# First superblock: the up-projection begun in halves of 256 columns for two chunks instead of four, with a new order of issue

## The chip, the cores and the metric

The kernel runs on one core of a Trainium2 chip. The metric is the time of one execution on the device, in microseconds (us). Before the change it is 470.64 us, the median of three runs (470.19 to 471.09).

## What is computed

The reference is a transformer block with adaptive layer norm: a linear-attention half and an MLP half, each with a residual, on 2048 tokens of width 512, in float32.

```python
sa, ca, ga, sb, cb, gb = split(silu(c) @ w_mod)            # six rows of 512
h = layernorm(x) * (1 + ca) + sa
q, k, v = h @ wqkv                                         # 32 heads of 16
phi(t) = concat(softmax(t @ w_phi), softmax(-t @ w_phi))   # per head, 32 features
o = phi(q) @ (phi(k).T @ v) / (phi(q) @ sum(phi(k)) + 1e-6)
x = x + ga * (o @ wo)
h = layernorm(x) * (1 + cb) + sb
y = layernorm(h)                                           # the MLP normalises again
x = x + gb * (gelu(y @ w1 + b1) @ w2 + b2)                 # w1: 512 x 1376
```

## The kernel before

Every product is taken as three float32r matmuls on high and low parts (`mm3`: high by high, high by low, low by high), so a tile of 128 rows with four slices of the contraction is 12 matmuls.

The tokens are 8 blocks of 256 (two tiles of 128). Two stages follow each other. In the first the weights are loaded and folded (`fold`), and block by block the keys, values and queries are projected (`pk`, `pv`, `pq`), the key features made (`ek`) and summed into one state (`pkv`, 32 small matmuls a tile). In the second the attention output of a block is formed and the MLP runs over four superblocks, each of two blocks (512 tokens). The names that matter here, for the stretch between the stages:

- `t` transposes the normalised query features of blocks 0 and 1 on TensorE (`qp`), and ScalarE copies them out (`qT`, `attn_t`, L800). `o` multiplies them with the state (`po`, L818), `w` with the output weights (`pw`, L844).
- `la`, `lb`, `lc` (L851 to L871) are the residual and the two layer norms of a tile. VectorE does sums, statistics and scalings on `pw`; ScalarE copies the residual out (`x1`) and writes the result `h2`; each reciprocal root (`rsb`, `rsc`) is one GpSimd operation between two VectorE ones.
- `y` (`attn_y`, L880) transposes `h2` of a block on TensorE (`yp`, 8 matmuls); ScalarE writes the high part (`yT0`), VectorE the low part (`yT1`).
- `u` (`up`, L916) is one chunk of the up-projection: 128 of the 1376 features for the 512 tokens of a superblock, 12 matmuls of 512 columns into `pg`; then the gelu on ScalarE and the split into `g`. `d` is a chunk of the down-projection (`py`, 12 matmuls).
- `w_prep` (L606) loads a pair of chunks of `w2` into `ws`, multiplies it on GpSimd, copies it on ScalarE (`w2a`, `w2b`) and subtracts on GpSimd. `w1` is prepared likewise (`w1s` to `w1`).

A chunk of the first superblock needs both blocks 0 and 1. For the first `AHEAD` chunks (L202) it is done in two halves, so that the half of block 0 can run before block 1 has its `yT`:

```python
n = 256 if b == 0 and fc < AHEAD else 512
for j in range(0, 512, n):
    if n < 512:
        nc.item(f"u{j // n}")
```

The halves are items `u0` and `u1`, whole chunks `u`. Both halves of a chunk write one PSUM bank, and its gelu follows the second.

What sets the order: the program first records every instruction into queues by part and item (`Later`, L220), and `issue` (L237) then emits them in the order of the table `ISSUE` (L87), one string for each of the 13 parts. `u0.p` is the TensorE part of the next `u0`, `.a` ScalarE, `.v` VectorE, `.g` GpSimd, `.s` a DMA on the queue of SyncE; a `-` takes the item from the part before, a `+` from the part behind. Each engine executes its instructions in that order and waits for what the next one needs. `SLOTS` (L46) says which of the 19 working buffers (`buf`), the 8 PSUM banks and the small tiles each new tile takes; a tile waits until the last user of its buffer is done. All matmuls, activations and transfers are recorded under one line, L217, so that the profile tells them apart by tile.

Of the kernel before, what the change touches and what calls it, by code (L numbers as in the profile page):

```python
# [59 lines left out]
    "mxk": "1010101110101010",  # L60
    "smk": "0110010111011011",
    "rck": "1010010111101101",
    "mxq": "10110010",
    "smq": "00000000",
    "rcq": "10100020",
    "den": "00101110",
    "rd": "10111011",
    "st6b0": "10100110",
    "stb0": "10111101",
    "veb0": "10010101",  # L70
    "rsb0": "11001011",
    "st6c0": "01000110",
    "stc0": "10111100",
    "vec0": "00100100",
    "rsc0": "00101000",
    "nmc0": "10010111",
    "st6b1": "11110101",
    "stb1": "10000110",
    "veb1": "11111110",
    "rsb1": "00010101",  # L80
    "st6c1": "10000001",
    "stc1": "10111010",
    "vec1": "00110110",
    "rsc1": "00100101",
    "nmc1": "00000111",
# [40 lines left out]
pk1.p -k0.v -k1.a --bg.g -k0.v -k1.v pk0.p h.a -v0.v v1.v k1.v -v0.a -k0.g +d0.s h.a k1.v ----e.s h.a h.a f.a -m0.p
--bg.g k0.v f.a -m1.p k1.v m0.p k1.v pv1.p +w1.s -k1.v +w1.s k1.a --v1.v f.g -v1.v k0.v v1.v k0.v f.g k1.v
""",
    """
pk1.p -v1.a -----e.v --k1.g ---bg.a --v1.a -k0.v -k0.a -k1.v pk0.p ----v0.v k1.v +lp0.s -k1.g -k0.v --v1.v --bg.g  # L130
-k0.v -m1.p w1.a k0.v m1.p k1.v -pv0.p w1.a d0.s v1.v k0.v w1.s -k0.g k0.v v0.v k1.v k0.v -v0.v pv0.p w1.g k0.a
-v0.a k0.v w1.g k0.v pv1.p k1.v v0.a +a0.v k1.a v0.v v1.v k1.v k0.g q1.p v1.a k1.v w1.a +a0.v k1.g ---v0.v m0.p
+a0.g m2.p m3.p w1.g kT.a d1.s d1.s z.p z.a kf.p +a0.g q0.p z.a q1.a a0.g q1.p a1.g a0.v -----e.v a0.v --bg.s q2.p
q1.a a1.g +a0.a kf.v a0.v q0.a a1.v q2.p a0.g a1.v a0.g a0.g +a0.g a0.v +a0.v q0.p a1.g a0.g a1.g a0.v a1.g a0.g
a1.v q4.p q0.a --bg.s x0.s q2.a a1.g +a0.g t01.p a1.g +a0.a t01.p t00.p t00.p +a0.v q4.p q4.a a1.g t01.a +a0.v t00.a
t01.a t00.a +a0.g q2.a o01.p q2.s o00.p w1.s t10.p q0.s o00.a t11.p o01.a +a0.g o00.v t10.p t11.p o01.v w00.p t10.a
+a0.v q4.a t11.a q4.s --bg.g +a0.v t10.a t11.a w1.a o11.p la00.v o10.p la00.a -bg.g w01.p x1.s o10.a la00.v o11.a
o10.v la00.v o11.v +a0.g -bg.a la00.v la00.v la00.g w11.p +a0.g la01.v +a0.g w1.g lb00.v la01.a +a0.v la01.v lb00.v
w10.p la11.v w1.s q1.s la01.v lb00.v la11.a la01.v la01.v +lp1.s la01.g w2.s la11.v -bg.g lb01.v q3.p la11.v lb01.v
la10.v +a0.g lb01.v la11.v la10.a lb00.v lb01.v la11.v lb00.g lb01.g q3.p la10.v la11.g lc00.v la10.v lc01.v la10.v  # L140
lc01.a la10.v la10.g lb11.v +a0.g lc00.a lb10.v q3.a y0.p q3.a lb11.v y0.p y0.a +a0.g lb10.v q3.s y0.a y0.v --bg.a
lb10.v y0.v
""",
    """
u0.p -w1.a -lb11.v -lb10.v -lb11.v a0.v -lb10.g -lb11.g u0.p a0.v ---bg.g -lc10.v -lc11.v a0.v a0.s -lc10.a a1.v
a0.s u0.p -lc11.a a0.s a1.v a0.s a1.g -y1.p -y1.p -y1.a u0.p --v0.v a0.v a1.g -y1.a -y1.v a0.s a1.g -y1.v a1.a a0.s
u1.p a0.s a1.g a0.s u1.p -w1.g +lp0.s u.a u.a u1.p u.a u.v a0.s u.a a1.v a0.s -w2.g d.p -w1.s u.a d.p u.v u.a d.p
u.v d.p a1.g a1.a d.p d.p -w2.a a1.v d.p a1.g d.p a1.v d.p x0.s a1.v u1.p -w2.g a1.v o01.p o00.p +a0.v d.p o00.a
a1.g -w2.s o01.a o00.v d.p a1.g a1.g +a0.g u.p a1.v o01.v u.a a1.g a1.g d.p a1.g w01.p a1.v u.a +a0.v u.a -w1.a u.v
u.a -w2.g a1.v d.p la01.v a1.s d.p a1.v la01.a a1.s w00.p u.v +a0.g -w2.a a1.s a1.v a1.s -w2.g la01.v a1.s a1.s  # L150
# [45 lines left out]
d.p u.v d.p d.p d.p u.p d.p u.a d.p u.a d.p u.v d.p u.p u.p u.a u.a u.v d.p u.a d.p u.a u.p u.v d.p u.a d.p u.a d.p  # L196
u.a u.a d.p u.a u.a u.a u.v d.p d.p d.p d.p d.p out.v d.p out.s d.p out.v d.p out.s d.p out.v d.p out.s out.v out.v
out.s out.s
""",
]  # L200
W2A = 6
AHEAD = 4  # L202
NT = 2
BUFS = 19
ALIGN = 64
NE = 2


# [963 lines left out]
```

## Time and profile before

| | us |
|---|---|
| median of three runs | 470.64 |
| the profiled execution | 470.68 |
| its span | 468.9 |
| TensorE busy | 462.5 (99%) |
| VectorE busy | 314.1 (67%) |
| GpSimd busy | 279.7 (60%) |
| ScalarE busy | 235.6 (50%) |

The ends of matmuls are modelled, so a busy TensorE may hold short waits; the chain of waits gives the dense rate. The stretch in which the two stages meet lies between 140 and 205 us of the span.

### The profile page before, as it was taken

The page shows a single profiled execution, that of the slowest core. Times are in us where ns is not written, and L with a number is a line of the kernel's source. Part 1 is how long each engine was busy: PE and PEld are TensorE (multiplying, and loading weights), DVE is VectorE, ACT ScalarE, POOL GpSimd, SP SyncE. Part 2 cuts the span into 40 slices and gives each one's busy share as a digit, 9 for nine tenths or more (in the row PEclk, how much of TensorE's full clock was granted, in tenths as well). Part 3 has the DMA queues.
Part 4 walks back from the last instruction along what each step waited for, and adds up shares of the span by engine and source line. Part 5 has one row for each costly group of instructions (what it writes and reads, how often), then busy time and mean ns, then how long its engine had stood idle before and what let it go on. Part 6 is the DMA issues. An engine that isn't in the chain of part 4 may idle for free.

```text
span 468.9 us, 8567 instructions
## 1 busy us (share of the span) xinstructions
PE 462.5 (99%) x3313; PEld 375.2 (80%) x3313; DVE 314.1 (67%) x610; ACT 235.6 (50%) x383; POOL 279.7 (60%) x233
## 2 busy tenths in 40 slices
PE   9999999999999999999999999999999999999996
PEld 5888888888878878988787878788788788788884
DVE  4999989998848389578885869795873282211113
ACT  2777686855541555758537672166533224422221
POOL 0485859879899989999879975663740010400000
PEclk9999999999999999999999999999999999999999
DMA  8999639636622446937636838168337205100002
GB/s 293 401 263 296 148 78 244 220 65 217 205 64 89 141 174 228 223 112 163 191 97 135 223 113 202 48 110 196 118 76 178 87 0 135 46 22 24 0 1 89
DMA packets 81033, 67.00 MB, mean 143 GB/s; under 512 B 52560, under 2 KB 68320, under 8 KB 80736
## 3 DMA queue, kind: packets, MB, share of 16 engines
q1 hardware_dynamic: 80992, 66.46, 50.1%
q8 instruction: 26, 0.43, 0.4%
q14 instruction: 15, 0.12, 0.1%
HBM read 44.41 MB, written 22.03 MB: 142 GB/s over the span
## 4 chain that ended last, share of the span: by engine, by line
PE 92%; DVE 3%; issue 1%; ACT 1%; DMA 1%; DVEq 0%; ACTq 0%
PE pg L217 26%; PE py L217 26%; PE pv L217 9%; PE pk L217 9%; PE pq L217 7%; PE pw L217 7%; PE warm L217 2%; PE pkv L217 2%; PE fold L217 1%; DVE pw L217 1%; PE po L217 1%; DMA pq_dram<-qs 1%; ACT qT L217 1%; DVE st6c L217 1%; PE zp L217 0%
## 5 line engine op out<-in xcount | busy, mean ns | idle before, releaser
L217 PE MATMUL pg<-yT,w 128*128 128x512 f32 (+1 forms) x528 | 115.5, 370 | 0.7 <-DVE yT L217 0.4
L217 PEld LDWEIGHTS pg<-yT,w 128*128 128x128 f32 x528 | 92.9, 188 | 18.2 <-DVE yT L217 0.6
L217 ACT ACTIVATE pg<-pg,blob 128x512 f32<-128x512 f32 x44 | 29.1, 661 | 106.5 <-PE pg L217 104.3
L217 DVE TENSOR_TENSOR g<-pg,g 128x512 fp32r<-128x512 f32 x40 | 27.2, 684 | 66.9 <-ACT g L217 66.7
L217 PE MATMUL py<-w2a,g 128*128 128x512 f32 x288 | 71.9, 392 | 0.0
L217 PEld LDWEIGHTS py<-w2a,g 128*128 128x128 f32 x288 | 53.5, 188 | 13.4 <-issue 1.6
L217 PE MATMUL py<-w2b,g 128*128 128x512 f32 x192 | 47.2, 390 | 0.0
L217 PE MATMUL pv<-wvh,hT 128*128 128x512 f32 x192 | 45.8, 392 | 0.0
L217 PE MATMUL pk<-wk,hT 128*128 128x512 f32 x192 | 45.6, 391 | 0.0
L217 PE MATMUL pw<-wo,oT 128*128 128x512 f32 x192 | 45.6, 390 | 0.0
L217 PE MATMUL pq<-wq,hT 128*128 128x512 f32 x192 | 45.2, 390 | 0.0
L217 POOL TENSOR_TENSOR ez<-eq,zb 128x1024 f32<-128x1024 f32 x15 | 36.4, 2440 | 13.2 <-PE pg L217 6.1
L217 PEld LDWEIGHTS py<-w2b,g 128*128 128x128 f32 x192 | 35.9, 188 | 8.1 <-issue 0.7
L217 PEld LDWEIGHTS pw<-wo,oT 128*128 128x128 f32 x192 | 35.9, 188 | 7.8 <-issue 0.4
L217 PEld LDWEIGHTS pq<-wq,hT 128*128 128x128 f32 x192 | 35.9, 188 | 7.4
L217 PEld LDWEIGHTS pv<-wvh,hT 128*128 128x128 f32 x192 | 35.7, 188 | 7.5
L217 PEld LDWEIGHTS pk<-wk,hT 128*128 128x128 f32 x192 | 35.8, 188 | 7.3
L217 POOL TENSOR_TENSOR ek<-ek,rck 128x1024 f32<-128x1024 f32 x16 | 31.0, 1947 | 4.3 <-ACT vf L217 1.6
L217 POOL TENSOR_TENSOR eq<-eq,rcq 128x1024 f32<-128x1024 f32 x15 | 28.9, 1939 | 0.2
L217 ACT ACTIVATE g<-pg 128x512 fp32r<-128x512 f32 x40 | 24.0, 599 | 9.5 <-DVE stc L217 2.8
L217 POOL TENSOR_TENSOR rsb<-veb,mhalf 128x1 f32<-128x1 f32 x16 | 8.8, 550 | 30.3 <-DVE veb L217 30.3
L217 POOL TENSOR_TENSOR yT<-yf,yT 128x256 fp32r<-128x256 f32 x24 | 17.1, 744 | 15.2 <-ACT yT L217 15.2
(154 smaller groups left out, 802.4 us busy)
## 6 DMA issues: line engine op xcount, KB each, us to landing
et_dram<-eb SPq DMA_DIRECT2D x48, 128.0 KB, 2.8
eT<-et_dram SPq DMA_DIRECT2D x12, 512.0 KB, 5.5
xt<-in_x SPq DMA_DIRECT2D x8, 512.0 KB, 6.4
wms<-in_wmodT SPq DMA_DIRECT2D x8, 512.0 KB, 5.9
x<-in_x SPq DMA_DIRECT2D x8, 512.0 KB, 3.8
out<-x SPq DMA_DIRECT2D x15, 256.0 KB, 2.1
nt_dram<-nb SPq DMA_DIRECT2D x24, 128.0 KB, 3.3
hd<-nt_dram SPq DMA_DIRECT2D x6, 512.0 KB, 4.2
```

Source lines behind the costliest of these rows:

```text
L217: return lambda *a, **k: self.later.hold(self.letter, lambda: f(*a, **k))
```

## The change

`AHEAD` goes from 4 to 2: chunks 2 and 3 of the first superblock are one item `u` with 12 matmuls of 512 columns instead of `u0` and `u1` with 12 of 256 each. TensorE has 48 matmuls of 256 columns less and 24 of 512 more. The work of the other engines is the same, but for two table loads less on ScalarE. The whole of `ISSUE` and of `SLOTS` is new.

```diff
 SLOTS = {
     "buf":
-    "32eg91ai750d4gf6cf8ehcd187ga30203dh540b52ca0i999hba44571a6i7b8gag3fii0729f4c2fe569d1ehch8d61bg59801c"
+    "cd732950ega7f8146ba9acbah2g53i18b8id6c71470ide31ac60h0gd354ch66b4e95391gi6g8b8f2h275f0i6aeacd471b3h2"
...
-AHEAD = 4
+AHEAD = 2
```

On TensorE, where the first superblock begins: `yp` are the transposes of block 0 (`h2_438`) and of block 1, `pg_506`, `pg_508`, `pg_517` are the chunks 0, 1 and 2. Before:

```order
L217 MATMUL yp_480<-blob_106,h2_438 128x128 x4
L217 MATMUL pg_506<-yT0_475,w1_376 128x256
...
L217 MATMUL pg_508<-yT0_475,w1_376 128x256
...
L217 MATMUL pg_517<-yT0_475,w1_376 128x256
...
L217 MATMUL yp_502<-blob_106,h2_499 128x128 x4
L217 MATMUL yp_503<-blob_106,h2_499 128x128 x4
```

After:

```order
L215 MATMUL yp_480<-blob_106,h2_438 128x128 x4
L215 MATMUL pg_506<-yT0_475,w1_376 128x256
...
L215 MATMUL yp_502<-blob_106,h2_499 128x128 x4
L215 MATMUL yp_503<-blob_106,h2_499 128x128 x4
L215 MATMUL pg_508<-yT0_475,w1_376 128x256
```

Three halves (36 matmuls) stood between the two groups of transposes; now one half (12 matmuls) does.

On GpSimd, around the layer norms of block 0: `rsb0_431` is the first reciprocal root, `ws_349` and `w2a_348` prepare `w2`, `w1_377` prepares `w1`, `dz`, `den` and `rcq` belong to the attention of block 2. Before:

```order
L217 TENSOR_TENSOR ez_523<-eq_515,zb_116 128x1024
L217 TENSOR_TENSOR ws_324<-ws_324,gbb_115 128x1024
L217 TENSOR_TENSOR ws_349<-ws_349,gbb_115 128x1024
L217 TENSOR_TENSOR dz_521<-dz_521,rcq_520 128x128
L217 TENSOR_TENSOR rsb0_431<-veb0_430,mhalf_108 128x1
L217 TENSOR_TENSOR den_524<-dz_521 128x64
L217 TENSOR_TENSOR den_524<-den_524,deps_109 128x64
L217 TENSOR_TENSOR w1_377<-w1s_386,w1_377 128x4x256
L217 TENSOR_TENSOR rsb1_464<-veb1_463,mhalf_108 128x1
```

After:

```order
L215 TENSOR_TENSOR ez_523<-eq_515,zb_116 128x1024
L215 TENSOR_TENSOR ws_349<-ws_349,gbb_115 128x1024
L215 TENSOR_TENSOR dz_521<-dz_521,rcq_520 128x128
L215 TENSOR_TENSOR w1_377<-w1s_386,w1_377 128x4x256
L215 TENSOR_TENSOR den_524<-dz_521 128x64
L215 TENSOR_TENSOR rsb0_431<-veb0_430,mhalf_108 128x1
L215 TENSOR_TENSOR den_524<-den_524,deps_109 128x64
L215 TENSOR_TENSOR ws_324<-ws_324,gbb_115 128x1024
L215 TENSOR_TENSOR rcq_520<-rcq_520,rd_525 128x128
L215 TENSOR_TENSOR rsb1_464<-veb1_463,mhalf_108 128x1
```

`w1_377` moved ahead of `rsb0_431`, and `ws_324` behind it, ahead of `rsb1_464`. By the new `SLOTS`, `ws_349` now takes the buffer that the first `qT` of block 0 held, so its load waits for the `po` matmuls that read that `qT`; the two `qT` of block 1 take the buffers of two `eq` tiles that the `qp` transposes read.

## Rows read from the trace of the kernel before

**Rows 1.** The page: busy us (share of the span) and instructions, by engine.

```profile
PE 462.5 (99%) x3313; PEld 375.2 (80%) x3313; DVE 314.1 (67%) x610; ACT 235.6 (50%) x383; POOL 279.7 (60%) x233
```

**Rows 2.** Stretches: busy us (instructions) by engine, granted clock, DMA share, GB/s.

```profile
24.39:140.00 115.61, 115.07 (x1486) 95.12 (x1486) 101.81 (x214) 74.35 (x122) 96.23 (x63) 1.00 0.61 178
140.00:189.00 49.00, 47.88 (x301) 39.10 (x300) 37.02 (x67) 23.86 (x39) 45.35 (x38) 1.00 0.49 159
205.00:340.00 135.00, 135.00 (x705) 108.38 (x704) 106.14 (x184) 75.65 (x114) 101.05 (x95) 1.00 0.57 143
```

**Rows 3.** The chain that ended last: start us, us, engine and tile.

```profile
86.16 5.69 PE pv L217 x24
...
189.66 5.75 PE pg L217 x48
195.41 6.52 PE py L217 x27
...
203.36 1.02 PE po L217 x32
...
216.21 2.72 PE pg L217 x12
```

**Rows 4.** Timeline of TensorE, 160 to 190: start, us, tile, count, idle before.

```profile
161.81 1.97 PE L217 MATMUL qp<-blob,eq 128*128 128x128 f32 x16
163.53 3.01 PE L217 MATMUL pw<-wo,oT 128*128 128x512 f32 x12
166.93 1.58 PE L217 MATMUL po<-qT,gab 64*32 64x256 f32 x32 [0.39 <-ACT qT L217]
168.44 8.46 PE L217 MATMUL pw<-wo,oT 128*128 128x512 f32 x36
176.73 5.61 PE L217 MATMUL pq<-wq,hT 128*128 128x512 f32 x24
...
184.33 4.46 PE L217 MATMUL pg<-yT,w 128*128 128x256 f32 x35 [0.43 <-DVE yT L217]
```

**Rows 5.** Timeline of ScalarE, 150 to 192.

```profile
165.79 1.57 ACT L217 ACTIVATE qT<-qp 128x512 f32<-128x512 f32 x3 [0.95 <-DMA pq_dram<-qs]
...
186.58 1.45 ACT L217 ACTIVATE h<-pw,nmc,rsc 128x512 f32<-128x512 f32 x2 [0.74 <-DVE nmc L217]
```

**Rows 6.** DMA of the tile ws, 135 to 190: issue to landing.

```profile
DMA to landing us min/median/max: 3.7/4.2/6.7
```

**Rows 7.** Timeline of GpSimd, 150 to 192.

```profile
164.79 4.73 POOL L217 TENSOR_TENSOR ws<-ws,gbb 128x1024 f32<-128x1024 f32 x2
169.48 0.46 POOL L217 TENSOR_TENSOR dz<-dz,rcq 128x128 f32<-128x128 f32 x1
170.98 0.56 POOL L217 TENSOR_TENSOR rsb<-veb,mhalf 128x1 f32<-128x1 f32 x1 [1.04 <-DVE veb L217]
171.50 0.29 POOL L217 TENSOR_TENSOR den<-dz 128x64 f32<-128x64 f32 x1
172.12 2.39 POOL L217 TENSOR_TENSOR w<-w1s,w 128x1024 fp32r<-128x1024 f32 x1
```

**Rows 8.** Timeline of VectorE, 150 to 192.

```profile
172.10 0.75 DVE L217 SCALAR_TENSOR_TENSOR pw<-pw,rsb,sbb 128x512 f32<-128x512 f32 x1
...
183.60 0.67 DVE L217 TENSOR_TENSOR yT<-yp,yT 128x512 fp32r<-128x512 f32 x1
...
185.14 1.31 DVE L217 STREAM_TRANSPOSE eb<-eq 128x512 f32<-128x512 f32 x2
```

**Rows 9.** Waits of the weight loads of TensorE, 0 to 24: us, times, longest.

```profile
PEld hp L217 <- DVE wk L217: 0.3, 1, 0.3
```

**Rows 10.** Timeline of GpSimd, 118 to 151: the last key product.

```profile
133.61 1.94 POOL L217 TENSOR_TENSOR ek<-ek,rck 128x1024 f32<-128x1024 f32 x1 [0.55 <-DVE rck L217]
135.51 1.06 POOL L217 TENSOR_TENSOR eq<-pq,mxq 128x512 f32<-128x512 f32 x1
```

**Rows 11.** Timeline of TensorE, 118 to 151: the last key sums.

```profile
135.34 1.91 PE L217 MATMUL pkv<-ek,vf 128*17 128x32 f32 x192
```

More of the change, by code (lines that the diff above doesn't have):

```diff
@@ L62 @@
[L62 to L85, printed above, removed]
+    "1764310451231425022252401576077241156424075126405067163024511345357630506022674244361260321756460306"
+    "43436630436342350610761761706701004214305670766775056067067162000003530",
+    "st6a": "00011110",
+    "sta": "10010101",
+    "vea": "00011000",
+    "rsa": "11110101",
+    "nma": "01100100",
+    "dz": "110110110",
+    "mxk": "0101010101101000",
+    "smk": "0110001110011100",
+    "rck": "0010101010010001",
@@ new lines @@
+    "mxq": "00000000",
+    "smq": "10111001",
+    "rcq": "01210110",
+    "den": "00001101",
+    "rd": "00100011",
+    "st6b0": "11011100",
+    "stb0": "10110011",
+    "veb0": "11111010",
+    "rsb0": "01001011",
+    "st6c0": "10011001",
+    "stc0": "11111101",
+    "vec0": "00111011",
+    "rsc0": "01010111",
+    "nmc0": "01010111",
+    "st6b1": "11101011",
+    "stb1": "10100010",
+    "veb1": "00101010",
+    "rsb1": "11111111",
+    "st6c1": "01001001",
+    "stc1": "01100110",
+    "vec1": "11100101",
@@ L86 @@
+    "rsc1": "11100011",
+    "nmc1": "00011001",
 }
@@ L134 @@
[L134 to L138, printed above, removed]
@@ new lines @@
++n.v ++s.v k1.v +n.a ++++s.v bg.a f.g +bg.v q1.a n.s
+""",
+    """
+pk1.p bg.a bg.s n.v ++s.v -e.g -k0.v n.a -bg.v +s.g -k0.v e.v pk0.p --k1.v +n.v n.v h.a n.v h.a -v1.a q0.p -k1.v n.s
+bg.a bg.g e.v n.s h.a n.s h.a --k1.g +v0.v -k1.v f.a n.s -k0.v +n.a q1.p +n.v -k0.v -k1.a f.g ++s.v +++s.v ++s.v
+-v1.v bg.v f.a bg.v bg.a k0.v f.g -e.v -m0.p -m1.p e.g bg.p pv0.p +n.v bg.a +n.a e.g bg.s n.s q0.a +n.v e.g -k0.a
+-k1.v +n.s e.a e.g +n.s pv1.p k1.v +n.s q1.a ++s.v ++s.g bg.s v0.a bg.s ++n.v -k0.v bg.s +n.s
@@ new lines @@
+-k1.v f.g k1.v -m0.p k1.a -m1.p +w1.s -k1.g m0.p ----e.s v1.a k1.v
+""",
+    """
+pk0.p +lp0.s w1.s --v1.v -k0.v --bg.g -k0.v -k1.v -k0.v pk1.p k0.v -k0.a -k1.g v1.v --v1.v k0.v -v0.v k0.v k0.v
+-m1.p w1.a -k0.v m1.p w1.s -pv0.p k0.a w1.g k1.v -k0.v v1.v -v1.v k0.v -k0.g k1.v d1.s pv1.p w1.a d0.s k1.v +a0.v
+w1.g k1.v k0.v pv0.p k1.a -v0.v +a0.v v1.a k0.g v0.v k1.v q1.p v0.v k1.v w1.a +a0.g v0.a k1.g -v0.a m0.p m2.p +a0.g
+d1.s m3.p d0.s kT.a w1.g z.p z.a kf.p q1.p +a0.g z.a w1.s a0.g q4.p a1.g a0.v a0.v q0.p a1.g a1.v a0.v q0.p -----e.v
@@ new lines @@
+w10.p la01.v +a0.g la11.v la01.v la01.v la11.a la01.g lb00.v -bg.g la11.v lb01.v q3.p la10.v la11.v lb01.v la10.a
+lb00.v la11.v lb01.v la10.v lb00.g la11.g lb01.v la10.v q3.p la10.v lc00.v lb01.g la10.v lc00.a la10.g lc01.v la11.v
+q3.a +a0.g lc01.a lb10.v --bg.a lb11.v y0.p lb11.v +a0.g y0.p lb10.v y0.a lb11.v q3.a y0.v y0.a q3.s lb11.v lb10.v
+lb11.g lb10.v y0.v
+""",
+    """
+u0.p -lb10.g -lc11.v -lc11.a -w2.g -lc10.v a0.v -lc10.a a0.v a0.v a0.s -y1.p a1.v a0.s -y1.p ---bg.g -y1.a u0.p a0.s
@@ new lines @@
+la11.v u.p la11.g lb10.v lb10.v lb10.g +a0.g lc10.v u.v xb.g lb11.v d.p u.a lb11.v u.p lc10.a lb11.v lb11.v +a0.g
+lb11.g lc11.v +a0.v lc11.a y1.v +a0.g yf0.a u.p +a0.g y1.v yf0.a +a1.v y1.s y1.s u.a yf0.g u.a y1.s u.v y1.s d.p u.a
++a1.v +a1.g u.a d.p u.v u.a +a0.g d.p u.a +a0.v d.p yf0.a y1.s yf0.a d.p +a1.g +a0.v d.p +a0.v +a0.s d.p yf0.g +a1.a
+++lp0.s d.p +a1.g +a0.s u.a u.a d.p u.a +a0.s u.a u.v yf0.g d.p +a0.s +a0.v yf0.g d.p yf1.a yf1.a +a1.g yf1.a d.p
+d.p yf1.a d.p out.v yf1.g +a1.a d.p out.v d.p out.s yf1.g +a0.s +a1.v yf1.g +a0.s yf1.g
@@ new lines @@
+""",
+    """
+u.p a1.v a0.s -xb.g a0.s +a0.v -out.s u.p u.a +a0.v u.a a1.g a1.v -out.v u.p u.a -out.v -out.s u.a a1.g a0.s u.v
+-out.s u.v a0.s a1.v d.p u.a u.p a1.v u.a u.v a1.g a1.g a1.g +a0.g a1.v d.p d.p +a0.g d.p a1.g d.p a1.g d.p o01.p
+o00.p a1.g d.p o00.a u.a d.p o00.v +a0.g a1.v u.p x0.s a1.v +a0.g +a0.a a1.v a1.s a1.s u.a +a0.v +a0.g +a0.a a1.s
+d.p a1.s d.p o01.a o01.v w01.p +a0.g a1.v u.a u.v a1.s u.a a1.s u.v a1.s w00.p la01.v a1.s +a0.v la01.v la01.v d.p
+la00.v d.p a1.s la01.v a1.s la00.v u.p +a0.v la00.v +a0.v d.p u.a la00.v +a0.v d.p u.a d.p la00.v la00.v +lp1.s
@@ new lines @@
+lb10.v lb10.v d.p lb11.v +a1.v u.p u.a u.a lb10.v lb11.v lb11.v u.v lb11.g +a1.g lc11.v d.p lb10.g d.p +a1.g lc10.v
+lc10.a d.p lc11.a y1.v +a1.g d.p u.a y1.v d.p y1.s
+""",
+    """
+o00.p o01.p -y1.s a1.a -y1.s -d.p -y1.s -u.a -u.p a1.v o01.a a1.v -y0.s o01.v -y1.s -u.v -d.p -u.a a1.v -d.p o00.a
+-d.p a1.g o00.v -d.p -d.p -yf0.a -u.a -d.p -u.a -xb.g a1.v w01.p -yf0.a -yf1.a -yf0.a -yf1.a -u.a -yf1.a -u.a -yf1.a
+a1.g -u.a -yf0.a -yf0.g w00.p la01.v -u.a a1.g -u.v -yf1.g -yf1.g -yf1.g -d.p -d.p -yf0.g -d.p -out.v a1.g -d.p
@@ new lines @@
+-yf0.g a1.v -d.p -out.s la00.v -yf0.g la01.v a1.g -yf1.g u.p -out.v a1.g la00.v -out.s u.p u.a a1.g u.a a1.v u.v
+la01.v u.p a1.v u.a a1.s u.a a1.s u.v a1.s -out.v la01.v d.p a1.s -out.v u.a d.p d.p d.p a1.v d.p u.a a1.v d.p
+la01.v u.v a1.s la01.g d.p la01.v a1.s d.p la00.v a1.s d.p -out.s la00.v lb01.v d.p a1.s la00.v lb01.v la00.g d.p
+la00.v u.p lb01.v lb00.v lb00.v a1.s a1.s lb01.v lb01.g -out.s u.p u.a u.a u.v lc01.v lb00.v lc01.a d.p u.a d.p u.a
+d.p u.v u.p lb00.v lb00.g lc00.v lc00.a y0.v y0.v o11.p o10.p y0.s y0.s d.p o11.a o10.a d.p u.a o10.v d.p x1.s u.a
@@ new lines @@
+o11.v y0.s d.p u.v y0.s u.p d.p u.a d.p u.a w10.p y0.s d.p la10.v w11.p la10.v la10.v la10.v u.v d.p la11.v d.p
+la11.v d.p la11.v d.p la11.v la10.v la11.v la11.v la11.g d.p la10.v la10.g d.p lb10.v u.p lb10.v lb10.v lb11.v
+lb10.v lb11.v lb10.g d.p lb11.v lb11.v lc10.v lb11.g lc10.a u.p lc11.v u.a y1.v lc11.a y1.v u.p yf0.a y1.s u.a y1.s
+u.a u.v y1.s u.a y1.s u.v d.p u.a d.p yf0.a d.p y1.s yf0.g d.p d.p u.a u.p u.v yf1.a d.p yf1.a yf1.g yf1.a d.p u.a
+yf0.g d.p u.a yf1.g d.p yf1.a u.a yf1.g d.p yf0.a u.a u.a yf0.g d.p u.a u.a yf0.a u.v yf1.g d.p yf0.g
@@ new lines @@
+""",
+    """
+u.p -d.p u.a -d.p u.p u.a u.v -out.v -out.s -d.p u.a d.p -out.v u.a -d.p -out.s u.v u.p d.p u.a d.p u.a d.p u.v d.p
+d.p d.p d.p u.p -d.p u.a d.p u.a d.p u.v d.p u.p d.p u.a d.p u.a d.p u.v d.p -out.v d.p -out.s u.p d.p u.a d.p u.a
+d.p u.v d.p d.p u.p d.p u.a d.p u.a d.p u.v d.p -out.v d.p -out.s d.p u.p d.p u.a u.p u.a u.v d.p u.a u.p u.a u.v
+u.p u.a u.a u.v d.p u.a d.p u.a d.p u.a u.a d.p u.a u.a u.a u.v d.p d.p d.p d.p d.p d.p d.p out.v d.p out.s d.p
+out.v d.p out.s d.p out.v d.p out.s out.v out.v out.s out.s
```

138 lines of the change are left out of this document (43 added, 95 removed).

## The prediction

> **What bounds the kernel now.** I read the busy times first: TensorE is busy 99% of the span, the next engine 67% [rows 1]. Then the stretches: from 205 to 340 us TensorE has no idle time at all, from 24 to 140 it loses 0.54 us, and from 140 to 189, where the attention of the first blocks leads over to the MLP, 1.12 us [rows 2]. So the time is TensorE's work plus what it waits, and a new order can gain little: only waits and work that TensorE no longer has. A busy TensorE can hide waits, so I took the dense rate from the chain: 12 matmuls of 512 columns take 2.72 us, 226.7 ns each, and 48 of 256 columns 5.75 us, 119.8 ns each [rows 3]. Where a row is longer than count times rate, it holds a wait.
>
> **The change part by part.** Durations come from the profiled execution of 470.68 us (span 468.9, 1.78 us around it), 0.04 us above the median of the three runs; I add to 470.68.
>
> *Halves made whole.* 48 matmuls of 256 columns go and 24 of 512 come: 24 x (2 x 119.8 - 226.7) ns = 0.31 us gained [rows 3], all on TensorE, which never has slack here. Both ends are near that.
>
> *Start.* The weight load of the transposes `hp` waits 0.3 us for VectorE before the first projections [rows 9]. The new order puts a warm-up matmul ahead and the last fold before `hp`, so this product is not waited for: 0.3 gained; between 0 and 0.3 if another load comes late in its place.
>
> *Key sums.* A group of 24 `pv` behind `pkv` takes 5.69 us, where 24 x 226.7 ns is 5.44: 0.25 for a change of form [rows 3]. The groups of `pkv` go from six to seven: 0.25 lost (0 to 0.25).
>
> *First down-projection.* 27 `py` took 6.52 us, 27 x 226.7 ns is 6.12: 0.40 of waiting for the first `g` [rows 3]. In the new order chunk 2 in full (2.72 us) stands before the first `py`, which covers it: 0.40 gained (0 to 0.40, as the gelu now also starts later).
>
> *The attention of block 1.* From 163.53 to 168.44 TensorE did 12 `pw` and 32 records of `po`: 4.91 us [rows 4]. Dense it is 2.72 + 1.02, the `po` by a group that doesn't wait [rows 3], = 3.74. So 1.17 us is wait, for `qT`, whose copy was held by a store of the tile that had its buffer [rows 5]. In the new `SLOTS` these copies take buffers that the `qp` themselves free. `qp` ends at 163.53, three copies take 1.57, so four are done by about 165.7, before `pw` ends at 166.25: the wait goes, 1.17 gained (0 to 1.17). This time isn't kept, because TensorE only arrives earlier at the layer norms, which is the next term.
>
> *The layer norms and the two groups of transposes.* This is where the change decides. Before: the 24 `pq` start at 176.73 and are dense until 182.17; then come 16 `yp` (0.87 us for eight, from the end of 35 halves at 188.79 to 189.66) and 48 matmuls of 256 columns, 7.49 us dense. The 48th was done at 189.66 + 12 x 0.1198 = 191.10, so 1.44 us of it was waiting [rows 3, 4]. Block 1's `h` was ready at 188.03 [rows 5], and TensorE, busy with three halves of block 0, wanted it only at 188.8: 0.8 us in hand, with 36 matmuls as cover.
>
> After: TensorE reaches the end of `pq` at 182.17 - 1.17 = 181.0, and its cover between the two transposes is 12 matmuls, 24 x 0.1198 = 2.87 us less. Does `h` come earlier? Its chain begins at the reciprocal root `rsb0` on GpSimd. Before, that ran at 170.98, and VectorE used it at 172.10, after other work [rows 7, 8]. After, three things stand before it: `ws_349`, one `dz` and `w1_377`. The load of `ws_349` can't be issued before the first `po` is over, 161.8 [rows 4]. A load of this tile takes 3.7 to 6.7 us, median 4.2 [rows 6]; with two stores right behind it I take 4.6: landed at 166.4. Then 2.37 (half of 4.73), 0.46, 2.39, 0.29 and 0.56 [rows 7]: `rsb0` is done at 172.45. VectorE waits for it and all its queue with it: the second tile's statistics, the residual copies on ScalarE that follow, and both `h`. From that multiplication to the first `yT` of block 0 VectorE was busy without a pause, 172.10 to 183.60, 11.5 us [rows 8]; the same list now starts 0.35 later, so block 0's first `yT` is subtracted from about 184.1, with the second close behind at 185.7, and its 12 matmuls end near 186.3. Block 1: before, the last scalar step stood behind two transposes `eb` (185.14 to 186.45) [rows 8], and `h` followed at 186.58 [rows 5]. The new order puts `eb` behind it, which lets `h` start some 0.7 earlier: ready at 188.03 - 0.7, about 187.35. TensorE waits from 186.3 to 187.35. Then 0.87 for `yp` and 36 halves, 4.31: 192.53. Against 191.10 that is 1.43 us lost, with the 1.17 of the term before already in it.
>
> Bounds of the two together: if all waits of this place stay as they were, -1.17; if the load takes 6.7 us, 2.1 more, +3.5. I take +1.43, which is nearest to the rows of both chains.
>
> The Trainium skill, "DMA: Bandwidth & Descriptors", section "Anatomy of one DMA — SWDGE (gpsimd) path", gives, for transfers that GpSimd issues, about 2.0 us plus bytes by 436 GB/s for a DMA; an estimate from that page for 512 KB is 3.2 us. No load of this tile was that short (3.7 at least [rows 6]), so the measurement decides. By the page the load would land at 165.05, `rsb0` would be done before VectorE can use it (171.3), the chain would be 1.15 us earlier, and the sum 470.2 instead of the one below.
>
> *The rest.* From 205 to 340 TensorE was never idle [rows 2]; the last superblock has no attention to wait for. I count 0 for the new order there (0 to +1.5; it can't be better than no idle time).
>
> **Sum.** 470.68 - 0.31 - 0.3 + 0.25 - 0.40 + 1.43 = 471.35; I say 471.3. What a measurement of this kernel can tell from no change is about 0.2%, 0.94 us. So the forecast is no change that can be told, on the slow side: small gains in many places, eaten by one new wait.
>
> **Rivals.**
>
> *The layer norms come early.* If GpSimd's queue doesn't hold `rsb0` (the load lands by 164.8, as early as that multiplication ran before), the chain is 1.15 earlier and TensorE's idle time falls to what it was: the term is between +0.3 and -1.17, and with -0.9 the time is 470.68 - 0.76 - 0.9 = 469.0. For it: GpSimd is free from about 163, since one subtraction was moved ahead of `ez`. Against it: the load waits for `po`, and 2.87 us of cover are gone whatever the load does. Chance 0.18.
>
> *The key sums come late: slower.* The last 64 of the last 192 `pkv` records need the last `ek` product; they were due at 135.34 + 1.27 = 136.6 [rows 11], and the product was done at 135.55, behind 0.55 us of idle time, with one `eq` subtraction of 1.06 behind it [rows 10]. The new order puts that subtraction ahead of it: from 133.06, when GpSimd was free, 1.06 + 1.94 give 136.06, while the matmuls, 0.3 earlier by the start, come at 136.3. Of 1.05 us of margin 0.24 is left, and the root that the product needs now stands behind two reductions on VectorE. If it is later than that, everything behind it waits, since `z`, the first `ez` and the 72 `pq` follow on TensorE: late by one or two such operations costs 1.06 to 2.1 us, 471.35 + 1.6 = 472.9 at the middle. For it: VectorE is busy 88% from 24 to 140 and GpSimd 83% [rows 2]. Against it: these reductions and the subtraction are moved, not new, and their sum ahead of the last product stays about the same. Chance 0.25, with late transfers of later blocks counted in.
>
> *The clock falls.* TensorE would be idle for some 4 us between 181 and 187.4. The granted clock is 1.00, the 2.4 GHz level, in every stretch, that with 1.44 us of waits included [rows 2]. Were it at 1.2 GHz after the waits, the 36 halves would take 4.31 more: 475.6. Chance 0.03. The Trainium skill, "TensorE: Matmul & The Clock Gate", section "What's actually happening", says that the clock depends on how busy TensorE was of late, which is why this is a rival; no row here shows a fall.
>
> *The forecast*: 0.54, on its own between 470.2 and 472.4.
>
> **How the numbers follow.** Of the forecast's 0.54, 0.33 lie within 0.2% of 470.64 (469.7 to 471.58), 0.19 above, 0.02 below. The early rival gives 0.14 faster and 0.04 the same; the late key sums 0.02 the same and 0.23 slower; the clock 0.03 slower. Together 0.16 faster, 0.39 the same, 0.45 slower. The range runs from 469.2, where about half of the early rival lies, to 473.3, which takes in the late key sums at their middle; 2 in 10 are left out.
>
> **What the profile after would show.** Right: `po` of block 1 follows `pw` without a wait for `qT`; GpSimd idle before `ws` with the DMA as releaser, `rsb` starting near 171.9; a wait of TensorE for `h` before the second `yp` of about 1 us and waits for `yT` before the first `pg`; `py` without a wait at its start; 24 more matmuls of 512 columns at 226.7 ns. Wrong: the second `yp` starts without idle time before it (then the early rival), TensorE idle before the last `pkv` (the late key sums), a granted clock under 1.00, or idle time of TensorE behind 205 us, where I count none.

## The result and the profile after

The changed kernel takes 471.57 us (median of 13 runs, 470.95 to 472.80), the kernel before, beside it, 470.38 (13 runs): a ratio of 1.0029, 95% interval 1.0021 to 1.0037. It is 1.2 us slower. The forecast was 471.3, no change that can be told, on the slow side. The time is right within 0.3 us; by the 0.2% bound the change is just told from none. As a difference it is less close: the sum makes the change +0.7 us, from 470.68, and the kernel before ran at 470.38 beside it. Below, a kernel's profile is that of one execution; this one took 471.57 us, span 469.7.

The page of the changed kernel, as in [rows 1], and two of its stretches, as in [rows 2]:

```profile
PE 461.9 (98%) x3289; PEld 373.3 (79%) x3289; DVE 316.0 (67%) x610; ACT 233.4 (50%) x381; POOL 280.3 (60%) x233
```

```profile
140.00:189.00 49.00, 47.02 (x297) 38.52 (x296) 38.86 (x69) 24.44 (x40) 46.66 (x37) 1.00 0.45 151
205.00:340.00 135.00, 134.87 (x730) 107.14 (x729) 103.57 (x177) 71.49 (x109) 100.55 (x95) 1.00 0.55 138
```

TensorE's idle time has grown where the stages meet, from 1.12 to 1.98 us, and 0.13 us has come up behind 205. The timeline of TensorE in the changed kernel, as in [rows 4], shows it:

```profile
165.94 1.09 PE L215 MATMUL po<-qT,gab 64*32 64x256 f32 x32
166.96 8.45 PE L215 MATMUL pw<-wo,oT 128*128 128x512 f32 x36
175.25 5.61 PE L215 MATMUL pq<-wq,hT 128*128 128x512 f32 x24
180.70 1.03 PE L215 MATMUL yp<-blob,h 128*128 128x128 f32 x8
182.97 2.08 PE L215 MATMUL pg<-yT,w 128*128 128x256 f32 x12 [1.24 <-ACT qs L215]
185.79 1.09 PE L215 MATMUL yp<-blob,h 128*128 128x128 f32 x8 [0.74 <-ACT h L215]
186.63 7.36 PE L215 MATMUL pg<-yT,w 128*128 128x256 f32 x48
...
199.27 1.23 PE L215 MATMUL py<-w2a,g 128*128 128x512 f32 x3
```

`po` of block 1 waits for nothing now. Between the end of the 24 `pq` and the end of 48 matmuls of 256 columns stand 16 `yp` and these 48, dense 0.87 + 0.87 + 48 x 0.1198 = 7.49 us. Before, it took from 182.17 to 189.42 + 12 x 0.1198 = 190.86, 8.69, so 1.20 of waiting; now from 180.69 to 186.63 + 36 x 0.1198 = 190.94, 10.25, so 2.76. I use this measure for every kernel below; the row of the kernel before that it needs beside [rows 4] is

```profile
189.42 5.99 PE L217 MATMUL pg<-yT,w 128*128 128x256 f32 x48
```

The row at 199.27 has a hidden wait: three `py` are 0.68 dense, and the next row begins 1.07 behind it.

ScalarE in the changed kernel, as in [rows 5]:

```profile
166.78 0.60 ACT L215 ACTIVATE x<-pw 128x512 f32<-128x512 f32 x1 [1.36 <-DVE pw L215]
...
181.83 0.60 ACT L215 ACTIVATE yT<-yp 128x512 fp32r<-128x512 f32 x1 [0.61 <-PE yp L215]
182.32 0.59 ACT L215 ACTIVATE qs<-pq 128x512 f32<-128x512 f32 x1
182.80 0.61 ACT L215 ACTIVATE yT<-yp 128x512 fp32r<-128x512 f32 x1
184.29 1.45 ACT L215 ACTIVATE h<-pw,nmc,rsc 128x512 f32<-128x512 f32 x2 [0.88 <-DVE nmc L215]
```

The first row is the residual copy `x1`, with which the layer norms begin. In the kernel before it was

```profile
168.27 0.58 ACT L217 ACTIVATE x<-pw 128x512 f32<-128x512 f32 x1
```

GpSimd in the changed kernel, as in [rows 7], and the load of `ws` on SyncE's queue:

```profile
164.21 2.41 POOL L215 TENSOR_TENSOR ws<-ws,gbb 128x1024 f32<-128x1024 f32 x1
...
166.99 2.40 POOL L215 TENSOR_TENSOR w<-w1s,w 128x1024 fp32r<-128x1024 f32 x1
...
169.59 0.57 POOL L215 TENSOR_TENSOR rsb<-veb,mhalf 128x1 f32<-128x1 f32 x1
```

```profile
157.50 0.41 SPq L215 DMA_DIRECT2D ws<-in_w  x1
```

Block 1's `h` is ready at 185.74, 2.29 us earlier than before, and the second transposes begin right behind it. `rsb` runs at 169.59, not near 171.9, because the load of `ws` was issued at 157.50, before any `po`: it landed at 162.27, 4.8 us later, and the multiplication stood behind `ez`, not behind the load.

### The profile page after: what moved, and what is told of

The parts are those of the page before. It is cut to its first block, busy times and chain, and to the rows that moved or that the text cites. A ratio compares the mean times of both kernels' runs of the same rounds, so it can differ in the third digit from the quotient of the medians.

```text
span 469.7 us, 8522 instructions
## 1 busy us (share of the span) xinstructions
PE 461.9 (98%) x3289; PEld 373.3 (79%) x3289; DVE 316.0 (67%) x610; ACT 233.4 (50%) x381; POOL 280.3 (60%) x233
## 4 chain that ended last, share of the span: by engine, by line
PE 90%; POOL 3%; ACT 2%; DVE 2%; DMA 2%; issue 1%; SPq 0%; DVEq 0%; ACTq 0%
PE py L215 23%; PE pg L215 21%; PE pv L215 9%; PE pk L215 9%; PE pq L215 9%; PE pw L215 8%; PE pkv L215 2%; PE warm L215 2%; DMA eT<-et_dram 2%; PE fold L215 2%; PE po L215 1%; POOL eq L215 1%; PE qp L215 1%; POOL w2b L215 1%; POOL ws L215 1%
## 5 line engine op out<-in xcount | busy, mean ns | idle before, releaser
L215 PEld LDWEIGHTS pg<-yT,w 128*128 128x128 f32 x504 | 91.4, 188 | 19.7 <-ACT qs L215 1.5
L215 POOL TENSOR_TENSOR eq<-eq,rcq 128x1024 f32<-128x1024 f32 x15 | 29.9, 2006 | 0.4
L215 ACT ACTIVATE h<-pw,nmc,rsc 128x512 f32<-128x512 f32 x16 | 12.2, 776 | 30.5 <-DVE nmc L215 30.5
```

Source lines behind the costliest of these rows:

```text
L215: return lambda *a, **k: self.later.hold(self.letter, lambda: f(*a, **k))
```

## The experiments

All but one were timed against the kernel before on the same chip. In the diffs on `ISSUE` only the items of the engine in question are shown.

**Two halves in the old order.** TensorE's items, in the kernel before:

```diff
-u0.p u0.p u0.p -y1.p -y1.p u0.p u1.p u1.p u1.p d.p
+u0.p u0.p -y1.p -y1.p u1.p u1.p u.p d.p
...
-AHEAD = 4
+AHEAD = 2
```

> The order and the buffers of the kernel before, with two chunks in halves instead of four and nothing else changed: chunks 2 and 3 run whole where their second halves ran, so 24 halves stand between the two groups of transposes instead of 36. Theory (cover): in the kernel before TensorE reached the second transposes at 188.52 us and h was there at 188.03, 0.49 us in hand; 12 halves less take 12 x 0.1198 = 1.44 us, so 0.95 us of waiting appear. Whole chunks give 0.31 back, and the 0.40 us wait at the first down-projection goes, since a chunk of 2.72 us stands ahead of it. Sum +0.2 to +0.3 us against before. Rival (the loss belongs to the new order, not to the shorter cover): no new wait before the second transposes, -0.7 us.

Measured: 473.67 us, ratio 1.0062 (1.0043 to 1.0081), a loss ten times the expected one. TensorE, timeline of an execution that took 471.62 us:

```profile
181.12 1.03 PE L215 MATMUL yp<-blob,h 128*128 128x128 f32 x8
...
187.03 0.98 PE L215 MATMUL yp<-blob,h 128*128 128x128 f32 x7 [0.34 <-ACT h L215]
188.26 0.39 PE L215 MATMUL pg<-yT,w 128*128 128x256 f32 x1 [0.25 <-ACT yT L215]
189.72 5.76 PE L215 MATMUL pg<-yT,w 128*128 128x256 f32 x35 [1.08 <-DVE yT L215]
```

The wait for `h` is there, but most of the waiting is behind the transposes: with no half of block 0 left, TensorE waits for block 1's own `yT`. By the measure above it waits 3.87 us (from 181.12 to 189.72 + 23 x 0.1198). So halves of block 0 are cover twice, ahead of the second transposes for `h` and behind them for `yT`. My theory had only the first. A second look at the same kernel, since its runs lay at two levels:

> The same kernel as the run of two halves in the old order, once more with a profile, because its runs had two levels, 471.6 and 473.6 to 474.2 us, and the profile was of the lower one. Theory (the clock): in an execution of the upper level the granted clock falls to the 1.2 GHz level for some us behind the waits between 182 and 190 us; some 2 us more. Rival: the granted clock stays at 1.00 there and a transfer or a wait elsewhere makes the difference.

This one execution took 472.20 us, between the levels, with the granted clock at 1.00, so there is no trace of the upper level. The mean granted clock of the six runs says more: it is 0.999 and 0.998 in the two at 471.52 and 471.62 us, and 0.995 or 0.996 in the four at 473.64 to 474.20, while no execution of the kernel before or of the changed one has less than 0.998. One fall like that of the moved loads below, 3.42 us at 0.50, takes 0.0036 off such a mean. So the clock did fall in the upper level, and the 2.0 to 2.7 us between the levels go with it; where it fell isn't shown. The waits of the trace above, 2.67 us more than before, less the 0.31 and the 0.40 that the expectation counts, make 2.0 us.

**More cover, new order.** TensorE's items, in the changed kernel:

```diff
-u0.p -y1.p -y1.p u0.p u1.p u1.p u.p
+u0.p u0.p -y1.p -y1.p u1.p u1.p u.p
```

> The changed kernel with one item of TensorE moved: block 0's half of chunk 1 (12 matmuls of 256 columns) goes ahead of the second transposes, so 24 halves stand between them instead of 12. Theory (cover): the first half ends at 184.89 us, 12 more end at 186.33, where h has been there since 185.74: the second transposes start at about 186.4 instead of 185.79 with 12 matmuls less behind them, 0.85 us gained: 470.7, +0.3 against before. Rival (given back): behind 205 us TensorE waits for the features of block 3, whose load landed at 227.0 us; if that load doesn't come earlier with TensorE, the wait there grows from 0.42 to 1.3 us and the time stays at 471.5.

Measured: 471.31 us, ratio 1.0025 (1.0015 to 1.0035): no gain. TensorE:

```profile
186.75 1.04 PE L215 MATMUL yp<-blob,h 128*128 128x128 f32 x8
188.03 0.38 PE L215 MATMUL pg<-yT,w 128*128 128x256 f32 x1 [0.25 <-ACT yT L215]
188.76 5.77 PE L215 MATMUL pg<-yT,w 128*128 128x256 f32 x35 [0.34 <-DVE yT L215]
```

The wait for `h` is gone as the theory says, and the same 12 matmuls are missing behind the transposes: 2.91 us in all against 2.76. Neither theory had this.

**Four halves, new order.** In the changed kernel, from the first superblock's `py3` on, banks 5 and 6 also change places:

```diff
-u0.p -y1.p -y1.p u0.p u1.p u1.p u.p
+u0.p u0.p u0.p -y1.p -y1.p u0.p u1.p u1.p u1.p
...
-AHEAD = 2
+AHEAD = 4
```

> The changed kernel with four chunks in halves again: 36 halves between the two groups of transposes, all else in the new order (two PSUM banks are exchanged from the first superblock's chunk 2 on, so that the third half has a free bank). Theory (cover): of the 24 halves added, 2.87 us, all beyond 0.87 us is more than the wait; the 0.74 us wait for h before the second transposes goes (0.87 with what lies around it), and the halves cost 0.31 more: -0.55 us against the changed kernel, +0.6 against before. Rival (cover isn't what is missing): the 0.31 alone, 0.3 us slower than the changed kernel, +1.5 against before.

Measured: 473.01 us, ratio 1.0063 (1.0051 to 1.0075), slower still. TensorE:

```profile
183.20 4.96 PE L215 MATMUL pg<-yT,w 128*128 128x256 f32 x36 [1.24 <-ACT qs L215]
187.99 1.04 PE L215 MATMUL yp<-blob,h 128*128 128x128 f32 x8
188.79 5.99 PE L215 MATMUL pg<-yT,w 128*128 128x256 f32 x48
...
202.09 0.50 PE L215 MATMUL py<-w2a,g 128*128 128x512 f32 x1 [2.30 <-DVE g L215]
```

At the transposes the theory holds: 36 and 12 halves leave 1.81 us of waiting, 0.95 less than 12 and 12. But the order of the other engines was made for whole chunks: `g` comes 2.30 us late for the down-projection. So the time says nothing on the cover; the rows do.

**The copy first.** ScalarE's items, in the changed kernel:

```diff
-y0.a q3.a y0.a
+q3.a y0.a y0.a
```

> The changed kernel with one ScalarE instruction moved: the copy qs of the last query projection goes ahead of the copy of block 0's first transposes. That copy frees the PSUM bank that the first chunk of the up-projection takes, and the trace puts 1.24 us of TensorE's idle time down to it. Theory (something else is right behind): the second matmul of that chunk needs VectorE's subtraction, which ended at 183.15 us and doesn't move; so only the first matmul comes earlier, 0.0 us gained: 471.5, and the idle time is put down to another wait. Rival (the copy is the wait): the chunk starts 0.5 us earlier, 12 halves and all behind them too: 471.0.

Measured: 471.39 us, ratio 1.0028 (1.0017 to 1.0040), as the theory says. TensorE:

```profile
182.80 0.38 PE L215 MATMUL pg<-yT,w 128*128 128x256 f32 x1 [0.75 <-ACT yT L215]
183.53 1.81 PE L215 MATMUL pg<-yT,w 128*128 128x256 f32 x11 [0.34 <-DVE vec L215]
186.09 1.09 PE L215 MATMUL yp<-blob,h 128*128 128x128 f32 x8 [0.75 <-ACT h L215]
```

The idle time put down to `qs` fell from 1.24 to 0.75, and the rest stands before the second matmul, for VectorE; the sum is 2.73 against 2.76. The copy was the last to come, with VectorE's subtraction right behind.

**The split and the load early.** In the changed kernel, VectorE's and SyncE's items:

```diff
-a1.v a1.v u.v
+u.v a1.v a1.v
...
-a1.s -w2.s -w2.s a1.s a1.s -w2.s
+a1.s a1.s a1.s -w2.s -w2.s -w2.s
```

> The changed kernel with two things moved. VectorE's split of the second gelu output g goes ahead of two reductions smq that wait for exponentials; and the two loads of eT for block 3 go ahead of two loads of ws on SyncE's queue. Theory: the second down-projection's wait at 200 us (0.28 us at its third matmul) is this split behind the reductions, and goes; the wait at po of block 3 (0.3 us beyond the dense rate at 227 us) is the load behind two others, and goes. Sum -0.3 to -0.6 us against the changed kernel: 471.0. Rival (something else is right behind): both waits keep their size under other names, 471.5.

Measured: 474.51 us, ratio 1.0085 (1.0054 to 1.0117): slower, but the six executions lie far apart. Three took 471.91 to 473.38 us, with a mean granted clock of 0.998, and three 475.63 to 476.68, with 0.995 or 0.996. The profile is of one of the latter, 476.29 us. In it both waits went (`po` of block 3 takes 1.02 us, its dense time), and a larger one came. GpSimd, TensorE, and two stretches (PE, PEld, DVE, ACT, POOL busy, then the granted clock):

```profile
227.09 2.40 POOL L215 TENSOR_TENSOR ws<-ws,gbb 128x1024 f32<-128x1024 f32 x1 [2.83 <-DMA ws<-in_w]
...
231.79 0.55 POOL L215 TENSOR_TENSOR rsc<-vec,mhalf 128x1 f32<-128x1 f32 x1
```

```profile
233.42 4.76 PE L215 MATMUL pw<-wo,oT 128*128 128x512 f32 x12 [2.13 <-DVE oT L215]
```

```profile
231.30:234.72 3.42, 1.30 (x5) 0.86 (x5) 2.26 (x5) 2.03 (x3) 3.34 (x3) 1.00 0.01 4
234.72:238.14 3.42, 3.42 (x9) 2.64 (x9) 2.39 (x4) 0.60 (x1) 2.18 (x2) 0.50 0.03 6
```

The load of `ws`, moved back by two transfers, holds GpSimd for 2.83 us; the reciprocal root `rsc` stands behind it, VectorE behind `rsc`, and TensorE behind VectorE. Then the granted clock falls to 0.50, the 1.2 GHz level, for 3.42 us, and from the start of the 12 `pw` to the next matmul, at 237.98, it is 4.56 us instead of the dense 2.72. This is the mechanism that I had forecast for `rsb`, at another place. Whether the load came in time in the three shorter executions isn't shown.

**Four more on GpSimd**, in the changed kernel:

```diff
+    nc.item("pad")
+    for j in range(4):
+        nc.gpsimd.memset(pad[:, j:j + 1], 0.0)
...
+-pad.g -pad.g -pad.g -pad.g
```

> The changed kernel with four tiny GpSimd operations more (writes of one column to an unused tile) at the start. In the changed kernel the span ends 1.47 us behind the landing of the last store, in the kernel before 1.03; the difference stands at GpSimd's last instructions, whose first began 0.38 us later than in the kernel before. GpSimd issues 329 instructions there, 332 before. Theory (the number of GpSimd's instructions decides): the end is 1.03 us again, -0.4: 471.1. Rival (the end follows the order, not the number): 1.47 stays, 471.5.

Measured: 470.79 us, ratio 1.0012 (1.0003 to 1.0021), 0.8 us faster than the changed kernel. The last work of VectorE and the span, of the changed kernel and of this one:

```profile
core 0 of [0], span 469.7 us
...
465.58 0.76 DVE L215 TENSOR_TENSOR x<-py,x 128x256 f32<-128x256 f32 x2 [0.47 <-PE py L215]
```

```profile
core 0 of [0], span 469.2 us
...
465.51 0.76 DVE L215 TENSOR_TENSOR x<-py,x 128x256 f32<-128x256 f32 x2 [0.47 <-PE py L215]
```

The work ends 0.07 us earlier, the span 0.5 us; the rest of the 0.8 is no more than the intervals leave open. Behind the last landing stand 1.03 us, as in the kernel before, instead of 1.47. Four writes that nobody reads make the kernel faster; what the number decides is in the last section.

**The padding and the split**, both from above, no transfer moved:

> The changed kernel with the four tiny GpSimd operations of the earlier run and with VectorE's split of the second g ahead of the two reductions, and no transfer moved. Theory: the end behind the last landing is 0.43 us shorter, as measured, and the wait of 0.4 us in the second down-projection goes without the harm that the moved loads did: -0.8 us against the changed kernel, 470.7, no difference from before. Rival (the split is needed no earlier): -0.4, 471.1.

Measured: 470.85 us, ratio 1.0011 (1.0002 to 1.0020), no more than the padding alone. The wait of 0.4 us at `py` is gone, and 0.34 us comes back in waits of 0.1 to 0.2 before `po` of block 3. That `po` itself (1.03 us) waits no longer, so by the rows 0.3 us are left over (33.63 us from the `py` at 199.51 to that at 233.14, with the padding alone 33.93), less than the medians can tell.

**The store early.** In the kernel before, ScalarE's and SyncE's items, around block 1's `qT`:

```diff
-o01.a t10.a q4.a t11.a q4.s
+o01.a q4.a q4.s t10.a t11.a
```

> The kernel before, with one ScalarE copy qs of the queries and the store that follows it moved ahead of the first qT copies of block 1. That store held the buffer that three qT copies need, and TensorE waited for them at the state product po of block 1: 0.96 us beyond its dense rate. Nothing else is changed, the four chunks in halves stay. Theory (kept): the layer norms begin with the result of the product behind po, so they come as much earlier as TensorE does, and the new order's gain here is a real one: -0.9 us against before, 469.4. Rival (not kept, as the prediction has it): TensorE only arrives earlier at the layer norms and waits there: 0.0, 470.3.

Measured: 470.09 us, ratio 0.9997 (0.9988 to 1.0006). It tells nothing: `po` waits as before (0.39 us idle), because the buffer is held by another store, the first of the three, issued 4.6 us before it lands. I had moved the wrong one.

**That and the start**, in the kernel before (TensorE's items):

```diff
--init.p fq.p -w2.p -w3.p fk.p sr.p fq.p fk.p h0.p fk.p h0.p -w4.p
+-init.p -w4.p fq.p -w2.p -w3.p fk.p sr.p fq.p fk.p fk.p h0.p h0.p
```

> The kernel before with the copy and store moved as in the run of the early store, and with TensorE's start in the order of the changed kernel: one warm-up matmul goes from behind the transposes hp to the first ones, and both groups of hp stand behind the third fold of the keys. Four chunks stay in halves. Theory (both gains add): -0.9 and -0.3 us, 469.1, faster than both kernels. Rival (the start isn't kept, since the first loads or VectorE set when the keys' products begin): as the run of the early store, 469.4.

Measured: 470.23 us, ratio 1.0000 (0.9991 to 1.0008). The start isn't faster: the weight load of the transposes `hp` still waits 0.32 us for VectorE's `wk`. Which other part of the new order it needs isn't shown.

**The buffer**, in the kernel before, one character of `SLOTS` (the tile `qT_459`):

```diff
-...i1ia4e7a...
+...i1ia2e7a...
```

> The kernel before with one buffer changed and nothing moved: one qT tile of block 1 takes the buffer of an eq tile, which the qp transposes read, instead of that of qs, whose store left the buffer only at 165.71 us. This is the same kind of choice that the changed kernel has there. The wait at po of block 1 (0.95 us beyond the dense rate) should go in either case. Theory (kept): the layer norms begin with the product behind po and come as much earlier: -0.9 us against before, 469.4, faster than both kernels. Rival (not kept, as the prediction has it): 0.0, 470.3, and the wait stands before the first up-projection instead.

Measured: 470.11 us, ratio 0.9999 (0.9990 to 1.0008). TensorE and ScalarE:

```profile
166.15 1.09 PE L217 MATMUL po<-qT,gab 64*32 64x256 f32 x32
...
181.67 1.09 PE L217 MATMUL yp<-blob,h 128*128 128x128 f32 x8 [0.60 <-ACT h L217]
...
189.07 5.99 PE L217 MATMUL pg<-yT,w 128*128 128x256 f32 x48
```

```profile
167.00 1.06 ACT L217 ACTIVATE w<-w1s 128x1024 fp32r<-128x1024 f32 x1 [1.01 <-DMA w1s<-in_w]
167.96 0.58 ACT L217 ACTIVATE x<-pw 128x512 f32<-128x512 f32 x1
```

The wait at `po` is gone and comes back in full: 2.11 us at the transposes (from the end of `pq`, 180.91) instead of 1.20. The prediction said that this time isn't kept, and the second row of ScalarE says why: the residual copy `x1` stands behind a copy of `w1` that waits for its load.

**The copy behind**, the buffer kept, ScalarE's items:

```diff
-w1.a la00.a o10.a o11.a
+la00.a o10.a o11.a w1.a
```

> The kernel before with the buffer changed as in the run of the buffer, and one ScalarE instruction moved: the copy of w1, which in that run waited for its load until 167.00 us, goes behind the first residual copy x1 and the two copies oT of block 1. In the run of the buffer the wait at po was gone (0.93 us) and came back before the first up-projection (0.91 us more), because x1, with which the layer norms begin, stood behind that copy and ended at 168.54 us as before. Theory (the chain of the layer norms begins at x1): x1 starts at 167.0 instead of 167.96, all layer norms are 0.9 us earlier, and the 0.9 us is kept: 469.4 us, -0.9 against before, faster than both kernels. Rival (VectorE's own work or another instruction is right behind): 470.1, the wait stays before the first up-projection.

Measured: 469.08 us (468.38 to 469.37), ratio 0.9974 (0.9963 to 0.9984): faster than both kernels. ScalarE and TensorE:

```profile
166.69 0.60 ACT L215 ACTIVATE x<-pw 128x512 f32<-128x512 f32 x1 [1.00 <-DVE pw L215]
...
168.14 1.07 ACT L215 ACTIVATE w<-w1s 128x1024 fp32r<-128x1024 f32 x1
```

```profile
180.61 1.03 PE L215 MATMUL yp<-blob,h 128*128 128x128 f32 x8
...
187.06 1.04 PE L215 MATMUL yp<-blob,h 128*128 128x128 f32 x8
187.85 5.99 PE L215 MATMUL pg<-yT,w 128*128 128x256 f32 x48
```

The chain of the layer norms moves with TensorE, and the wait at the transposes is 1.20 again, with all 0.9 us kept.

What TensorE waits between the end of `pq` and 48 matmuls of 256 columns, by the rows above:

| kernel | halves of block 0 ahead of / behind the second transposes | waits, us |
|---|---|---|
| before | 36 / 12 | 1.20 |
| before, buffer | 36 / 12 | 2.11 |
| before, buffer and copy behind | 36 / 12 | 1.20 |
| before, two halves | 24 / 0 | 3.87 |
| changed | 12 / 12 | 2.76 |
| changed, more cover | 24 / 0 | 2.91 |
| changed, four halves | 36 / 12 | 1.81 |

The ends of `pq` that these waits start from are, in the order of the rows, 182.17, 180.91, 180.60, 181.12, 180.69, 181.12 and 180.93.

## Why the prediction was right or wrong

The terms, measured as differences of the two profiles:

| term | predicted | measured | from |
|---|---|---|---|
| halves made whole | -0.31 | -0.31 | 24 fewer matmuls by count, at the same dense rates |
| start | -0.3 | -0.3 | first `pk` at 17.47 for 18.25, less 0.47 (below) |
| key sums, down to `po` | +0.25 | +0.3 | first `pk` to the last `pkv`: 117.46 for 117.09; `pkv` to `po`: 25.34 for 25.44 |
| `po` of block 1 | -1.17 | -0.97 | first `po` to the 36 `pw`: 6.69 for 7.66 |
| layer norms and transposes | +2.60 | +1.56 | 2.76 for 1.20 |
| first down-projection | -0.40 | 0 | 0.4 us at 200 now, 0.4 at 195 then |
| behind 205 | 0 | +0.4 to +0.5 | idle before `po` of block 3, small waits |
| end of the span | not named | +0.43 | 1.47 for 1.03 |

Together about +1.2 us, what the medians show. The two profiled executions differ by 0.89 only, mostly because of the clock at the start (last section). The prediction's 1.44 us of waiting before, and its 0.8 us in hand, mix starts of the chain with starts of the timeline; by the timeline alone they are 1.20 and 0.49.

*Right in kind, the size off: the layer norms.* That less cover between the transposes turns into waits for `yT` and `h`, and that these eat more than `po` gains, is what happened. But the chain began earlier than I had it. The failed step is "The load of `ws_349` can't be issued before the first `po` is over, 161.8". I had taken the buffer of the wrong tile: it is a later tile of `ws` that takes the buffer of the first `qT`, and what the words ahead of the prediction say of `ws_349` there is wrong. Its load was issued at 157.50. So `rsb` was not late, the early rival's mechanism came true, and its time did not: the cover that was argued against it there was missing, 12 halves ahead of the transposes and 12 behind, where before had 36 and 12. That halves are needed behind the transposes too I had not seen; the two runs with 24 and none showed it.

*Wrong for the changed kernel: "This time isn't kept".* The prediction lets TensorE only arrive earlier at the layer norms. But `x1` starts at 166.78 instead of 168.27, 1.49 us earlier, and the 36 `pw` behind `po` at 166.96 instead of 168.44, 1.48 us earlier: the chain of the layer norms came forward with TensorE, and by `h` even by 2.29. So the time was kept there, and spent behind it: by the run with four halves 0.95 us of the 1.56 is the shorter cover, and the other 0.61 comes with the new order, whose first `pg` waits 1.24 us where the kernel before has two waits of 0.73 together. In the kernel before with one buffer changed the step holds, and there it hangs on one copy of `w1` ahead of `x1`, as the run with that copy moved shows; in the changed kernel none stands there.

*Wrong: the first down-projection.* A whole chunk does cover the first `g`. The second `g` is then late, since VectorE's split of it stands behind two reductions that wait for exponentials until 197.01. With the split moved the wait was gone, and most of it came back before `po` of block 3.

*Wrong: nothing behind 205, and the end.* The load of `eT` for block 3 landed late for `po` in the changed kernel's profile; moving it forward cured that and broke GpSimd's queue. The end of the span I had not looked at: the run with four more GpSimd operations gives 0.43 us back.

*The rivals.* The key sums were not late: the last `pkv` begin 2.82 us behind the 12 `pq` ahead of them, before 2.81. The clock stayed at 1.00 with 1.98 us of idle time in 49; in the run with the moved loads it did fall behind a wait of 2.13 us, and by the mean clock it fell in four of six executions with two halves in the old order, whose trace shows 3.87 us of waiting without a fall. So that rival was a real one. The Trainium skill, "TensorE: Matmul & The Clock Gate", section "What's actually happening", ties the clock to how busy TensorE was of late, and the run with the moved loads agrees: the fall comes 1.3 us behind the end of that wait. The estimate of 3.2 us for a load of 512 KB by the Trainium skill ("DMA: Bandwidth & Descriptors", section "Anatomy of one DMA — SWDGE (gpsimd) path", for transfers by GpSimd) was again short of the measured 4.8 us on SyncE's queue.

So the time came out right partly because errors cancelled: the layer norms cost 1.04 us less than forecast, while `po` gained 0.2 less, the 0.40 counted at the down-projection did not come, and 0.4 behind 205 and 0.43 at the end were not in the sum. That the kernel before ran 0.3 us below the 470.68 that the sum starts from was luck as well.

## What to carry to other kernels

Work that covers a wait has to be counted on both sides of the instruction that waits: for the data it needs, and for the engines that make its result ready for the next one. An idle time named in a profile has another right behind it as often as not, so a gain upstream is kept only when the chain that ends last begins with it; look there for the instruction of another task at the head of a queue, as the copy of `w1` ahead of `x1`. In an order made for one form, undoing a part alone tells little by its time, but its rows tell which wait it was. And where the runs of a kernel lie at two levels, look at their granted clock first: a profile of the one level doesn't explain the median of the other.

## What the runs showed of the hardware

TensorE's first matmuls run at half rate for a time that differs from run to run. The weight loads of the warm-up, kernel before and changed kernel:

```profile
5.35 0.34 PEld L217 LDWEIGHTS warm<-ones 128*128 128x128 f32 x1 [0.52 <-issue]
6.21 0.34 PEld L217 LDWEIGHTS warm<-ones 128*128 128x128 f32 x1 [0.52 <-issue]
```

```profile
6.09 0.19 PEld L215 LDWEIGHTS warm<-ones 128*128 128x128 f32 x1 [0.41 <-issue]
6.52 0.19 PEld L215 LDWEIGHTS warm<-ones 128*128 128x128 f32 x1 [0.24 <-issue]
```

They follow each other by 0.86 us, and later by 0.43, in a factor of two like that of the two clock levels. The trace's record of the granted clock begins at 6.92 us in the one and at 5.97 in the other, and in the profiles of the twelve runs between 3.79 and 6.81. Half of 0.95 us is the 0.47 taken off above; differences of that size between single executions are chance. The other profiles bear the half out. The start of the first `pk`, less half of the time at which the record begins, is 14.48 us, within 0.01, in all seven profiles of the changed kernel and its variants, and 14.79 or 14.80 in four of the six with the old start; in the other two the transposes `hp` wait 0.37 and 0.61 us for VectorE. So the new start is worth 0.31 us.

The end of the span depends on how many instructions GpSimd has. Behind the landing of the last store stand 1.46 or 1.47 us in the four profiles whose trace has 329 of them, 1.38 in the one with 330, and 1.03 in the nine with 332 or 333. Where there are 329 or 330, it is always the 325th that is late: it stands behind the landing and begins 0.38 or 0.39 us after the one ahead of it, where 0.08 or 0.09 is usual. With 332 and 333 the 325th lies before the landing, where GpSimd only waits. Why the 325th is late isn't shown.
